# Retention and a tanh-shrink MLP on one core: the first eight steps in another hand-written order

## The chip, the core and the metric

The kernel runs on one core of a Trainium2 chip. The core has a matrix engine (TensorE, PE in the profile, with its weight loads shown as PEld), three engines for elementwise work (VectorE, DVE; ScalarE, ACT; GpSimd, POOL) and a sync engine (SP) that here only issues DMAs. Every engine works off its own instruction list in order and waits for others by semaphores. The metric is the device time of one launch in microseconds (us), smaller is better. With the kernel before, four runs had a median of 696.73 us (695.07 to 699.09).

## The reference

```python
# q, k, v: (4, 8, 768, 64); w_in: (512, 2048); w_out: (2048, 512)
def _attn_ref(q, k, v):
    B, H, S, D = q.shape
    gamma = 1.0 - 2.0 ** (-5.0 - np.arange(H, dtype=np.float32))
    scale = 1.0 / np.sqrt(D)
    state = np.zeros((B, H, D, D), dtype=np.float32)
    y = np.zeros_like(q)
    for t in range(S):
        state = gamma[None, :, None, None] * state + np.einsum('bhd,bhe->bhde', k[:, :, t], v[:, :, t])
        y[:, :, t] = scale * np.einsum('bhd,bhde->bhe', q[:, :, t], state)
    return y.astype(np.float32)

# x: attention output as (3072, 512)
def _moe_ref(x, w_in, w_out):
    h = x @ w_in
    g = h - np.tanh(h)
    return (g @ w_out).astype(np.float32)
```

All inputs and the output are float32 or wider; the weights arrive as 64-bit floats and are converted on the chip.

## The kernel before

The 3072 tokens are 24 chunks of 128 (six chunks to a batch element). Each chunk goes through the attention in chunked form: powers of gamma are multiplied into q and v, k and q are transposed, products of k with v (the state's increment) and of k with q (the scores) are formed, the scores are masked, and outputs are summed from state and scores in PSUM and copied to `xT`, the transposed input of the MLP. The MLP runs in steps: a step is a pair (n, m2), 256 tokens by 256 columns of the hidden layer. It has an up-projection (two halves of 128 hidden columns), a chain of elementwise work for h - tanh(h) (a polynomial where h is small, and a choice between the two), and a down-projection (two halves of 128 tokens). Weights come in 32 blocks, alternating four blocks of w_in and four of w_out; each is loaded as 64-bit words and turned into float32 by bit operations on VectorE, ScalarE and GpSimd.

From step 8 on a loop sets the order, and from step 32 on both projections use a form with seven products in place of eight. The first eight steps are different: with them go the attention of chunks 0 to 7, the loads of chunks 0 to 8, and the conversion of weight blocks 0 to 11. Their order is a string of 367 single operations, `order` (lines 892 to 913), that is worked off from left to right; `pieces` (line 858) says what each name calls. Since every engine keeps the order in which its instructions are written, the string fixes the order on each engine and on SP's queue. The number behind the colon is a chunk c, a weight block i or a step s, and a last letter D, P or A gives VectorE, GpSimd or ScalarE as the engine.

- SP: `Lk Lq Lv` load k, q, v of a chunk (lines 255, 260; one DMA of 256 KB); `W` loads a weight block (line 154 for w_out, one DMA of 512 KB; line 159 for w_in, three DMAs). There are two buffers for k, two for q and four for v, given out in the order of the loads, so a load can wait in the queue until the older user of its buffer is done.
- TensorE: `x` sets a number of warm-up blocks of 128 columns that the next piece writes first (line 233); `t`, `T` transpose k and q (298); `p` makes the products, the k-v half at line 343, the scores at 349; `b` makes the outputs from state and scores (398), `r` the rest of them; `u`, `v` are the two halves of an up-projection (464); `o0`, `o1` those of a down-projection (531).
- VectorE: `z`, `Z` the two halves of the state (367 to 373), `m` the mask (356), `D1` to `D4` the bit operations of a weight block (191 to 201), `f0` to `f4` the products of the shrink (844 to 854).
- ScalarE: `c`, `C` copy the transposes out (310, 307), `e` copies four single columns of the outputs to `seen` (428), which `r` then waits for, `y` copies the outputs to `xT` (444), `A`, `l` take the high and low words of a weight block (175, 183), `au` to `alarge` the functions of the shrink (836), `E` keeps a finished half of a down-projection (545).
- VectorE or GpSimd: `s`, `w` multiply the powers of gamma into q and v (282), `F`, `G` end the conversion of a weight block (208, 217). A block is converted in the order A, l, D1 to D4, F, G.

What waits for what, where it matters here: `T` needs `s`, the first half of `p` needs `w` and k, its second half `c` and `C`; `b` needs `z` and `m` of its chunk; `u` and `v` of a step need `y` of its two chunks and `G` of one block each; `o` needs `f4` and `G` of two blocks.

Of the kernel before, what the change touches and what calls it, by code (L numbers as in the profile page):

```python
# [22 lines left out]
A = 0.00694305119022808  # L23
# [8 lines left out]
def kernel(  # L32
# [857 lines left out]
    if w_out.dtype != F32:  # L890
        rooms += [xp.tile([P, 2, 2 * BANK], U32, tag="xT", name=f"raws_{i}") for i in range(3)]
    order = """
    Lk:0 Lq:0 s:0D x:9 t:0 c:0 Lv:0 x:3 T:0 C:0 Lk:1 Lq:1 w:0D p:0 W:0 Lv:1 t:1 z:0 s:1P Z:0
    m:0 x:2 b:0 Lq:2 Lv:2 Lq:3 e:0 w:1D s:2D c:1 A:0 T:1 Lk:2 C:1 r:0 x:1 p:1 D1:0 z:1 T:2 m:1
    s:3D D2:0 Z:1 y:0 b:1 t:2 W:1 Lk:3 e:1 w:2P r:1 D3:0 C:2 l:0 c:2 p:2 D4:0 F:0P G:0P Lv:3
    y:1 z:2 m:2 A:1 T:3 b:2 t:3 Z:2 D1:1 D2:1 l:1 D3:1 D4:1 u:0 W:3 Lq:4 c:3 W:2 Lk:4 e:2 C:3
    r:2 y:2 w:3P p:3 l:3 A:3 Lv:4 F:1D z:3 Lv:5 Lq:5 Lk:5 m:3 G:1P b:3 s:4P e:3 A:2 v:0 r:3
    Z:3 D1:3 D2:3 w:4P W:5 Lv:6 ath:0 y:3 au:0 T:4 t:4 c:4 C:4 aq0:0 D3:3 D1:2 aq1:0 D4:3 D2:2
    alarge:0 l:2 F:3P f0:0 D3:2 v:2 p:4 f1:0 u:2 f2:0 s:5P G:3P au:2 ath:2 Lq:6 z:4 m:4 aq0:2
    Z:4 t:5 T:5 c:5 C:5 f3:0 Lk:6 A:5 D4:2 f4:0 w:5D F:2D f0:2 f1:2 D1:5 G:2P v:1 b:4 s:6P  # L900
    aq1:2 f2:2 w:6P p:5 e:4 r:4 z:5 f3:2 m:5 D2:5 u:1 W:4 D3:5 y:4 T:6 A:4 l:5 t:6 v:3 D1:4
    D4:5 D2:4 b:5 F:5D W:6 Lq:7 c:6 C:6 ath:1 l:4 D3:4 au:1 G:5D D4:4 e:5 aq0:1 p:6 r:5
    alarge:1 aq1:1 y:5 alarge:2 A:6 Lv:7 Lk:7 F:4D W:7 W:8 u:3 G:4P W:11 W:9 W:10 o0:0 s:7P
    m:6 f0:1 z:6 Z:6 f1:1 Lq:8 au:3 f4:2 D1:6 f2:1 A:7 aq0:3 t:7 D1:7 o1:0 T:7 f3:1 v:4 u:4
    l:6 aq1:3 D2:6 b:6 C:7 c:7 D2:7 f4:1 D3:6 ath:3 f0:3 D4:6 f1:3 w:7P f2:3 f3:3 D3:7 p:7
    F:6P G:6P e:6 l:7 D4:7 F:7D r:6 au:4 u:5 A:11 ath:4 m:7 y:6 G:7P v:5 alarge:3 f4:3 z:7
    aq1:4 au:5 aq0:4 o0:1 E0:1 f0:4 f1:4 f2:4 D1:11 o1:1 b:7 o0:2 ath:5 aq0:5 alarge:5 A:10
    aq1:5 e:7 E1:1 l:11 l:10 alarge:4 r:7 y:7 o1:2 f3:4 D2:11 Z:7 D1:10 D3:11 D2:10 D4:11
    F:11D f0:5 f1:5 f2:5 G:11D D3:10 D4:10 f4:4 f3:5 o0:3 A:8 F:10P D1:8 u:6 G:10D D2:8 v:6
    A:9 D1:9 D2:9 f4:5 D3:9 D4:9 D3:8 au:6 ath:6 aq0:6 aq1:6 E0:3 f0:6 l:9 o1:3 u:7 v:7 E1:3  # L910
    f1:6 f2:6 f3:6 D4:8 au:7 aq0:7 ath:7 alarge:6 l:8 F:9P G:9P f0:7 o0:4 aq1:7 F:8P o1:4 o0:5
    o1:5 E0:5 alarge:7 Lk:8 Lv:8 W:12 f4:6 f1:7 W:13 f2:7 f3:7 G:8D f4:7 W:14 E1:5
    """
    for piece in order.split():
        kind, at_ = piece.split(":")
# [200 lines left out]
```

## Time and profile before

| what | value |
|---|---|
| median of 4 runs | 696.73 us (695.07 to 699.09) |
| the profiled execution, its own time | 695.07 us |
| its span in the profile | 693.2 us |
| instructions | 16487 |
| first matmul of step 8 | 85.47 us after the span's start |
| granted TensorE clock in every stretch of 20 us | 1.00 |
| DMA, mean over the span | 86 GB/s (59.95 MB) |

The span is what the profiler sees between the first and the last instruction; the time has some 1.9 us around it. A share of busy time is a mean over the whole span, and the first eight steps are only its first eighth: the views by window and the timeline are the ones to read here. In a line of the timeline stand start and length in us, engine, line of the kernel, operation, the tiles written and read, their shape and the number of instructions, and in brackets the idle time of the engine before it with what ended that. Matmuls overlap each other, so their cost is read from start to start.

### The profile page before, as it was taken

The numbers are of one execution on the slowest core, as the hardware profiler recorded it, in microseconds if no ns is written. First come the engines' busy times: TensorE is split into PE (matmuls) and PEld (weight loads), VectorE is DVE, ScalarE is ACT, GpSimd is POOL, SyncE is SP. The second block draws the span as 40 slices with busy tenths as digits, with TensorE's granted clock in tenths as the row PEclk, the third lists the DMA queues.
The fourth block names the chain that finished last, engine by engine and source line by source line (L and its number), as shares of the span: only waits on it lengthen the run. The fifth ranks groups of instructions, "written<-read, shape, count | busy, mean of one in ns | idle before, by whom it ended". The sixth has DMA issues, their size and how long they took to land.

```text
span 693.2 us, 16487 instructions
## 1 busy us (share of the span) xinstructions
PE 686.1 (99%) x6540; PEld 572.7 (83%) x6540; DVE 524.0 (76%) x894; ACT 432.5 (62%) x818; POOL 347.7 (50%) x517
## 2 busy tenths in 40 slices
PE   8999999999999999999999999999999999999997
PEld 6776666667666767789999999999999999999996
DVE  4899999988988965487777676677676776766775
ACT  3787677767767665555665555655556655556653
POOL 1632454455544767878753354453544543544333
PEclk9999999999999999999999999999999999999999
DMA  9991278878968566400000000000000000000001
GB/s 237 239 293 48 66 181 223 206 175 243 210 189 228 143 162 192 124 32 1 1 1 22 11 1 31 1 1 31 1 1 31 1 8 24 2 16 17 1 16 46
DMA packets 119548, 59.95 MB, mean 86 GB/s; under 512 B 101680, under 2 KB 112560, under 8 KB 119472
## 3 DMA queue, kind: packets, MB, share of 16 engines
q1 hardware_dynamic: 116880, 50.21, 28.0%
q10 hardware_dynamic: 2592, 8.69, 3.4%
q8 instruction: 51, 0.84, 0.5%
q14 instruction: 25, 0.20, 0.1%
HBM read 35.83 MB, written 14.68 MB: 73 GB/s over the span
## 4 chain that ended last, share of the span: by engine, by line
PE 95%; DVE 1%; SPq 1%; issue 1%; DMA 1%; ACT 1%; POOL 0%; POOLq 0%; DVEq 0%; ACTq 0%
PE h L778 29%; PE h L464 16%; PE o L531 16%; PE fast_t L669 10%; PE y L669 8%; PE fast_o L669 8%; PE y L398 4%; PE s L349 2%; PE s L343 2%; PE kqTp L298 1%; DMA v<-in_v_dram 1%; SPq L260 0%; SPq L255 0%; SPq L159 0%; DVE g L523 0%
## 5 line engine op out<-in xcount | busy, mean ns | idle before, releaser
L477 ACT ACTIVATE th<-h 128x512 f32<-128x512 f32 x64 | 38.2, 598 | 141.5 <-DVE h L795 141.5
L620 POOL TENSOR_TENSOR s<-g 128x128 f32<-128x128 f32 x64 | 29.3, 457 | 192.2 <-DVE g L523 186.4
L464 PE MATMUL h<-xT,w 128*128 128x256 f32 x512 | 117.7, 382 | 0.0
L531 PE MATMUL o<-w,g 128*128 128x512 f32 x256 | 116.5, 596 | 0.0
L464 PEld LDWEIGHTS h<-xT,w 128*128 128x128 f32 x512 | 95.9, 190 | 21.3 <-issue 9.1
L531 PEld LDWEIGHTS o<-w,g 128*128 128x128 f32 x256 | 47.5, 190 | 46.2 <-issue 43.0
L778 PEld LDWEIGHTS h<-xT,w 128*128 128x128 f32 x512 | 76.8, 191 | 8.4 <-ACT fast_head L783 1.0
L523 DVE COPY_PREDICATED g<-large,th 128x512 f32<-128x512 int32 x88 | 74.0, 841 | 8.9
L793 DVE TENSOR_TENSOR h<-h,fast_head 128x256 f32<-128x256 f32 x64 | 27.7, 432 | 68.1 <-PE h L778 66.9
L778 PE MATMUL h<-xT,w 128*128 128x128 f32 x512 | 78.3, 275 | 0.2 <-ACT fast_head L783 0.2
L502 DVE TENSOR_TENSOR th<-h,th 128x512 f32<-128x512 f32 x88 | 60.1, 683 | 17.5 <-ACT th L475 16.2
L515 DVE SCALAR_TENSOR_TENSOR g<-q,h 128x512 f32<-128x512 f32 x64 | 44.0, 688 | 36.3 <-ACT q L491 34.8
L778 PE MATMUL h<-x,w 128*128 128x128 f32 x448 | 68.3, 275 | 0.0
L483 ACT ACTIVATE q<-u,tab 128x512 f32<-128x512 f32 x88 | 63.8, 725 | 1.8
L491 ACT ACTIVATE q<-u,tab 128x512 f32<-128x512 f32 x88 | 63.6, 723 | 0.0
L506 DVE SCALAR_TENSOR_TENSOR h<-q,h 128x512 f32<-128x512 f32 x88 | 60.8, 691 | 2.6 <-ACT q L483 2.6
L208 POOL TENSOR_TENSOR low<-low,power 128x512 f32<-128x512 f32 x26 | 34.6, 1330 | 56.1 <-DVE power L201 48.4
L492 ACT ACTIVATE large<-u,tab 128x512 f32<-128x512 f32 x88 | 62.6, 712 | 0.0
L778 PEld LDWEIGHTS h<-x,w 128*128 128x128 f32 x448 | 59.0, 192 | 0.0
L783 ACT COPY fast_head<-h 128x512 f32<-128x512 f32 x64 | 37.5, 586 | 20.3 <-PE h L778 20.3
L522 DVE TENSOR_TENSOR g<-g,u 128x512 f32<-128x512 f32 x64 | 49.1, 768 | 0.0
L788 POOL TENSOR_TENSOR fast_head<-fast_head 128x256 f32<-128x256 f32 x64 | 46.8, 731 | 1.2 <-ACT fast_head L783 1.2
(197 smaller groups left out, 1496.6 us busy)
## 6 DMA issues: line engine op xcount, KB each, us to landing
rows<-apart ACTq DMA_DIRECT2D x16, 512.0 KB, 4.8
k<-in_k_dram SPq DMA_DIRECT2D x24, 256.0 KB, 4.2
q<-in_q_dram SPq DMA_DIRECT2D x24, 256.0 KB, 4.8
v<-in_v_dram SPq DMA_DIRECT2D x24, 256.0 KB, 5.6
raw<-in_moe_w_out_dram SPq DMA_DIRECT2D x12, 512.0 KB, 4.6
out_dram<-sum SPq DMA_DIRECT2D x22, 256.0 KB, 2.0
raw<-in_moe_w_in_dram SPq DMA_DIRECT2D x14, 256.0 KB, 4.1
raw<-in_moe_w_in_dram SPq DMA_DIRECT2D x28, 128.0 KB, 3.9
```

The costliest lines, as they stand in the source:

```text
L464: nc.tensor.matmul(hp, w1[:, c, ts(2 * m2 + i, P)], xT[n // 2][:, c, ts(n % 2, TH)], start=(begins and c == 0), stop=(c == NC - 1), skip_g ...
L483: nc.scalar.activation(q0, shrinking[n, m2][0], AF.Square, bias=bias0)
L491: nc.scalar.activation(q1, u, AF.Square, bias=bias1, scale=math.sqrt(A))
L492: nc.scalar.activation(large, u, AF.Relu, bias=bias_m)
L502: nc.vector.tensor_tensor(th, hp, th, op=ALU.subtract)
L506: nc.vector.scalar_tensor_tensor(hp, in0=shrinking[n, m2][2], scalar=C0, in1=hp, op0=ALU.add, op1=ALU.mult)
L522: nc.vector.tensor_tensor(flat, src, u, op=ALU.mult)
L523: nc.vector.copy_predicated(flat, large.bitcast(I32), th)
L531: nc.tensor.matmul(o_p[n, j], gT[n, m2][:, i, ts(j, P)], w2[:, 2 * m2 + i], start=(first and i == 0), stop=(last and i == 1))
L669: nc.tensor.matmul(accs[n][k], left[k - 1], right, start=first and k in (1, 6, 7, 4), stop=last, skip_group_check=True)
L778: nc.tensor.matmul(hps[n, m2][:, ts(PLACE[k], P)], s_of[m2][k - 1][:, c], x_of[n][k - 1][:, c], start=(k == 1 and c == 0), stop=(c == 1), ...
L788: nc.gpsimd.tensor_tensor(odd_room[1], first[:, :2], first[:, 3:1:-1], op=ALU.add)
```

## The change

The string `order` is replaced by another with the same 367 operations. Their places differ, and some go to another queue or engine: `Lk:0` from SP's queue to ScalarE's; `s:1 s:7 w:3 w:4 F:6 F:9 F:10 G:0 G:1` from GpSimd to VectorE; `w:5 F:2 F:4 F:5 F:7 G:5 G:10` from VectorE to GpSimd. Nothing else in the kernel is touched.

```diff
--- before.py
+++ after.py
@@ -890,26 +890,26 @@
     if w_out.dtype != F32:
         rooms += [xp.tile([P, 2, 2 * BANK], U32, tag="xT", name=f"raws_{i}") for i in range(3)]
     order = """
-    Lk:0 Lq:0 s:0D x:9 t:0 c:0 Lv:0 x:3 T:0 C:0 Lk:1 Lq:1 w:0D p:0 W:0 Lv:1 t:1 z:0 s:1P Z:0
-    m:0 x:2 b:0 Lq:2 Lv:2 Lq:3 e:0 w:1D s:2D c:1 A:0 T:1 Lk:2 C:1 r:0 x:1 p:1 D1:0 z:1 T:2 m:1
-    s:3D D2:0 Z:1 y:0 b:1 t:2 W:1 Lk:3 e:1 w:2P r:1 D3:0 C:2 l:0 c:2 p:2 D4:0 F:0P G:0P Lv:3
-    y:1 z:2 m:2 A:1 T:3 b:2 t:3 Z:2 D1:1 D2:1 l:1 D3:1 D4:1 u:0 W:3 Lq:4 c:3 W:2 Lk:4 e:2 C:3
-    r:2 y:2 w:3P p:3 l:3 A:3 Lv:4 F:1D z:3 Lv:5 Lq:5 Lk:5 m:3 G:1P b:3 s:4P e:3 A:2 v:0 r:3
-    Z:3 D1:3 D2:3 w:4P W:5 Lv:6 ath:0 y:3 au:0 T:4 t:4 c:4 C:4 aq0:0 D3:3 D1:2 aq1:0 D4:3 D2:2
-    alarge:0 l:2 F:3P f0:0 D3:2 v:2 p:4 f1:0 u:2 f2:0 s:5P G:3P au:2 ath:2 Lq:6 z:4 m:4 aq0:2
-    Z:4 t:5 T:5 c:5 C:5 f3:0 Lk:6 A:5 D4:2 f4:0 w:5D F:2D f0:2 f1:2 D1:5 G:2P v:1 b:4 s:6P
-    aq1:2 f2:2 w:6P p:5 e:4 r:4 z:5 f3:2 m:5 D2:5 u:1 W:4 D3:5 y:4 T:6 A:4 l:5 t:6 v:3 D1:4
-    D4:5 D2:4 b:5 F:5D W:6 Lq:7 c:6 C:6 ath:1 l:4 D3:4 au:1 G:5D D4:4 e:5 aq0:1 p:6 r:5
-    alarge:1 aq1:1 y:5 alarge:2 A:6 Lv:7 Lk:7 F:4D W:7 W:8 u:3 G:4P W:11 W:9 W:10 o0:0 s:7P
-    m:6 f0:1 z:6 Z:6 f1:1 Lq:8 au:3 f4:2 D1:6 f2:1 A:7 aq0:3 t:7 D1:7 o1:0 T:7 f3:1 v:4 u:4
-    l:6 aq1:3 D2:6 b:6 C:7 c:7 D2:7 f4:1 D3:6 ath:3 f0:3 D4:6 f1:3 w:7P f2:3 f3:3 D3:7 p:7
-    F:6P G:6P e:6 l:7 D4:7 F:7D r:6 au:4 u:5 A:11 ath:4 m:7 y:6 G:7P v:5 alarge:3 f4:3 z:7
-    aq1:4 au:5 aq0:4 o0:1 E0:1 f0:4 f1:4 f2:4 D1:11 o1:1 b:7 o0:2 ath:5 aq0:5 alarge:5 A:10
-    aq1:5 e:7 E1:1 l:11 l:10 alarge:4 r:7 y:7 o1:2 f3:4 D2:11 Z:7 D1:10 D3:11 D2:10 D4:11
-    F:11D f0:5 f1:5 f2:5 G:11D D3:10 D4:10 f4:4 f3:5 o0:3 A:8 F:10P D1:8 u:6 G:10D D2:8 v:6
-    A:9 D1:9 D2:9 f4:5 D3:9 D4:9 D3:8 au:6 ath:6 aq0:6 aq1:6 E0:3 f0:6 l:9 o1:3 u:7 v:7 E1:3
-    f1:6 f2:6 f3:6 D4:8 au:7 aq0:7 ath:7 alarge:6 l:8 F:9P G:9P f0:7 o0:4 aq1:7 F:8P o1:4 o0:5
-    o1:5 E0:5 alarge:7 Lk:8 Lv:8 W:12 f4:6 f1:7 W:13 f2:7 f3:7 G:8D f4:7 W:14 E1:5
+    Lq:0 Lk:0A x:9 t:0 Lv:0 c:0 Lv:1 Lk:1 s:0D x:3 T:0 C:0 w:0D Lq:2 p:0 Lq:1 W:0 z:0 W:1 Lv:2
+    m:0 x:2 b:0 e:0 t:1 Z:0 w:1D c:1 s:1D Lk:2 r:0 s:2D y:0 T:1 C:1 A:0 w:2P x:1 p:1 z:1 D1:0
+    Lq:3 D2:0 T:2 m:1 b:1 A:1 C:2 Lk:3 l:1 e:1 Lv:3 t:2 c:2 Z:1 D3:0 r:1 D1:1 l:0 D2:1 p:2
+    D4:0 F:0P s:3D m:2 z:2 D3:1 G:0D w:3D T:3 Z:2 D4:1 F:1D y:1 b:2 e:2 C:3 t:3 W:3 Lq:4 s:4P
+    W:2 Lk:4 c:3 G:1D u:0 A:3 D1:3 r:2 y:2 A:2 p:3 z:3 Lv:4 m:3 Z:3 v:0 D2:3 D1:2 D2:2 T:4
+    D3:3 D3:2 t:4 C:4 w:4D c:4 b:3 D4:3 e:3 D4:2 l:3 r:3 y:3 Lq:5 au:0 aq1:0 ath:0 p:4 v:2
+    Lk:5 F:3P z:4 Lv:5 W:5 s:5P W:7 Z:4 m:4 f0:0 G:3P Lk:6 w:5P alarge:0 aq0:0 t:5 A:5 T:5 c:5
+    u:2 Lv:6 Lq:6 l:2 F:2P W:4 f1:0 b:4 G:2P C:5 p:5 s:6P f2:0 D1:5 f3:0 e:4 ath:2 au:2 r:4
+    f4:0 z:5 aq1:2 aq0:2 m:5 f0:2 Lq:7 Lk:7 W:11 Lv:7 W:6 W:10 W:9 Lq:8 Lv:8 y:4 W:8 w:6P v:1
+    A:4 t:6 T:6 D2:5 f1:2 u:1 C:6 D3:5 D1:4 c:6 l:5 b:5 D4:5 D2:4 F:5P f2:2 au:1 p:6 e:5 f3:2
+    D3:4 r:5 m:6 G:5P D4:4 z:6 aq1:1 y:5 l:4 F:4P G:4P Z:6 alarge:2 alarge:1 s:7D aq0:1 ath:1
+    v:3 u:3 T:7 t:7 o1:0 f4:2 f0:1 o0:0 w:7P A:7 D1:7 D2:7 f1:1 l:7 c:7 C:7 ath:3 au:3 b:6
+    D3:7 f2:1 A:6 aq0:3 D1:6 f3:1 aq1:3 e:6 p:7 r:6 D4:7 f0:3 f1:3 u:4 z:7 f2:3 F:7P Z:7 D2:6
+    f3:3 D3:6 v:4 f4:1 l:6 au:4 u:5 y:6 m:7 alarge:3 D4:6 G:7P b:7 F:6D G:6P ath:4 A:11 v:5
+    e:7 r:7 o1:1 o0:1 D1:11 aq1:4 alarge:4 aq0:4 A:10 l:10 au:5 E1:1 f0:4 l:11 y:7 f1:4 D1:10
+    o0:2 D2:11 D2:10 D3:10 D4:10 f2:4 f3:4 f4:3 D3:11 D4:11 E0:1 o1:2 aq0:5 alarge:5 ath:5
+    aq1:5 F:11D G:11D f0:5 f1:5 f2:5 f3:5 F:10D A:9 G:10P f4:4 v:7 u:7 o1:3 D1:9 ath:7 au:7
+    A:8 f0:7 D2:9 l:8 f4:5 D3:9 D1:8 D2:8 alarge:7 o0:3 E0:3 l:9 aq0:7 v:6 E1:3 D3:8 u:6 f1:7
+    D4:9 D4:8 o1:4 aq1:7 au:6 ath:6 aq0:6 F:9D f0:6 f2:7 aq1:6 o0:4 o1:5 f1:6 Lk:8 W:12 W:13
+    F:8P o0:5 E1:5 G:8D alarge:6 W:14 f3:7 f2:6 f3:6 f4:7 f4:6 G:9P E0:5
     """
     for piece in order.split():
         kind, at_ = piece.split(":")
```

Taken apart, the beginnings of four of the lists (old, then new):

```
SP      Lk0 Lq0 Lv0 Lk1 Lq1 W0 Lv1 Lq2 Lv2 Lq3 Lk2 W1 Lk3 Lv3 W3 Lq4 W2 Lk4 Lv4 Lv5 Lq5 Lk5 W5 Lv6 Lq6 Lk6 W4
        Lq0 Lv0 Lv1 Lk1 Lq2 Lq1 W0 W1 Lv2 Lk2 Lq3 Lk3 Lv3 W3 Lq4 W2 Lk4 Lv4 Lq5 Lk5 Lv5 W5 W7 Lk6 Lv6 Lq6 W4
TensorE x9 t0 x3 T0 p0 t1 x2 b0 T1 r0 x1 p1 T2 b1 t2 r1 p2 T3 b2 t3 u0 r2 p3 b3 v0 r3 T4 t4 v2 p4 u2 t5 T5 v1 b4 p5 r4 u1 T6 t6
        x9 t0 x3 T0 p0 x2 b0 t1 r0 T1 x1 p1 T2 b1 t2 r1 p2 T3 b2 t3 u0 r2 p3 v0 T4 t4 b3 r3 p4 v2 t5 T5 u2 b4 p5 r4 v1 t6 T6 u1
ScalarE c0 C0 e0 c1 A0 C1 y0 e1 C2 l0 c2 y1 A1 l1 c3 e2 C3 y2
        c0 C0 e0 c1 y0 C1 A0 A1 C2 l1 e1 c2 l0 y1 e2 C3 c3 A3 y2
VectorE s0 w0 z0 Z0 m0 w1 s2 D1:0 z1 m1 s3 D2:0 Z1 D3:0 D4:0 z2 m2 Z2 D1:1
        s0 w0 z0 m0 Z0 w1 s1 s2 z1 D1:0 D2:0 m1 Z1 D3:0 D1:1 D2:1 D4:0 s3 m2 z2 D3:1 G0 w3 Z2
```

## The prediction

> **What bounds the kernel now.** I read the engines' busy shares first, then the shares of the chain that ended last.
>
> ```profile
> PE 686.1 (99%) x6540; PEld 572.7 (83%) x6540; DVE 524.0 (76%) x894; ACT 432.5 (62%) x818; POOL 347.7 (50%) x517
> ...
> PE 95%; DVE 1%; SPq 1%; issue 1%; DMA 1%; ACT 1%; POOL 0%; POOLq 0%; DVEq 0%; ACTq 0%
> ```
>
> TensorE is the bound, so an order can only take away or add time in which TensorE waits. The windows show where such time can be (stretch, its length, then busy us and instructions of PE, PEld, DVE, ACT, POOL, then granted clock, DMA share, GB/s):
>
> ```profile
> 0.00:20.00 20.00, 17.50 (x393) 12.48 (x393) 9.83 (x20) 8.93 (x23) 4.81 (x8) 1.00 0.90 233
> 20.00:40.00 20.00, 19.60 (x409) 16.26 (x406) 18.49 (x34) 15.30 (x40) 11.99 (x11) 1.00 0.97 271
> 40.00:60.00 20.00, 20.00 (x314) 16.00 (x314) 19.15 (x34) 15.89 (x37) 7.11 (x6) 1.00 0.68 181
> 60.00:80.00 20.00, 20.00 (x124) 12.08 (x123) 18.46 (x35) 14.11 (x29) 3.85 (x3) 1.00 0.21 70
> ```
>
> For 40 us the DMA engines are full: the load order is a queue for one resource. From 20 us on VectorE is nearly full too. TensorE's waits:
>
> ```profile
> PE kqTp L233 <- DVE w L116: 1.4, 1, 1.4
> PE s L349 <- ACT kqT L310: 0.7, 1, 0.7
> PE y L398 <- DVE state L369: 0.3, 1, 0.3
> PE y L398 <- DVE a L356: 0.2, 1, 0.2
> ```
>
> From the timeline, the issue of W:1, the copy c:2, the second half of p:2 that waits for it, the outputs b:3, and w:4 on GpSimd:
>
> ```profile
> 11.54 2.77 SPq L159 DMA_DIRECT2D raw<-in_moe_w_in_dram  x3
> ...
> 17.11 0.57 ACT L310 COPY kqT<-kqTp 128x512 f32<-128x512 f32 x1
> ...
> 17.73 0.69 PE L349 MATMUL s<-kqT 64*64 64x64 f32 x32 [0.69 <-ACT kqT L310]
> ...
> 24.23 0.46 PE L398 MATMUL y<-kqT,state 64*64 64x64 f32 x16 [0.26 <-DVE state L369]
> ...
> 28.59 1.04 POOL L282 TENSOR_TENSOR v<-v,tab 128x512 f32<-128x512 f32 x1 [2.73 <-DMA v<-in_v_dram]
> ```
>
> **How much there is to win.** Step 8's first matmul starts at 85.47 us. I add up the TensorE work before it at its pace when nothing is waited for (start to start): 64 transposes of 0.109, 128 up matmuls of 0.216, 48 down matmuls of 0.430, 32 small ones in 0.46, 15 warm-up blocks of 0.107. With the warm-up counted twice, as each of its blocks is two instructions, that is 72.75 us. TensorE started at 1.45, so 11.3 us are over: 2.5 by 6.9 us (the cold start: a 512-column matmul took 853 ns there, half as much later), 4.8 from there to u:0 at 20.46, 2.8 to 46.53, 1.1 after that. Most of it is the 0.15 to 0.2 us of each change between small and large matmuls, which every order pays. Two pieces stand out, 0.91 over at p:2 and 0.86 over at b:3. More than about 2.5 us cannot be had.
>
> **The change, step by step.** The operations are the same 367; queues and engines differ. Landing times of before come from the trace's landing records: k:0 4.59, v:0 6.33, k:1 7.26, q:1 8.02, W:0 10.62, v:1 11.67, v:2 13.86, q:3 14.51, k:2 15.35, W:1 18.48, k:3 19.02, q:4 23.17, W:2 25.42. So a k or v costs the stream about 1.1 us, a q 0.85, a weight block 1.7 or more. Durations start to start: VectorE 0.60 for a product of two tiles, 0.35 for a bit operation or half a state; ScalarE 0.5 to 0.6 a copy; GpSimd 1.04 a scale, 1.27 an F or G.
>
> *Start, to 8.8 us: 0.* k:0 goes to ScalarE's queue behind the table (issue 0.43 us), q:0 is first on SP. TensorE's warm-up ends at 5.45 either way, and k:0 needs to land by then; alone on its queue, issued at 1.2 with before's 3.85 us, it lands at 5.0. ScalarE has nothing before c:0 at 6.45. If it lands 0.5 late, 0.5 is lost.
> The Trainium skill, "DMA: Bandwidth & Descriptors", section "Queues, rings and completion order", says the rows of the queues are served in turn by the same 16 engines, so a second queue adds no bandwidth; by that rule k:0 would share with v:0 and land some 0.5 us later than on a queue of its own, where the trace of before has only the table on that queue.
>
> *q:2 before q:1.* There are two q buffers; q:1 now waits in SP's queue for s:0 (over at 6.2), with W:0, W:1 and all later loads behind it. q:2's issue ahead fills SP until about 5.4, so this costs under 0.8, and nothing while the stream has a backlog.
>
> *p:1: -0.3.* v:1 lands at 7.3 in place of 11.67; q:1 at about 10.4. w:1, s:1 on VectorE end at 11.7, T:1 at 12.2, C:1 12.9, p:1's second half starts at 12.9 against 13.15.
>
> *b:1 to p:2: +0.5.* z:1, D1:0, D2:0, m:1 stand in a row on VectorE: 13.6+0.35+0.35+0.35+0.68 = 15.35, so b:1 ends at 15.7 (before 15.45). W:1's three DMAs now stand before v:2, k:2 and q:3 on SP: those land at 15.1, 16.2, 17.1 at the costs above, 17 for k:2 by the pace after 15 us. t:2 ran at 15.48, now 16.3. On ScalarE A:1 stands before C:2, l:1, e:1, c:2; with W:1 at 15.2 they end at 17.9, p:2 at 18.5 against 18.36.
>
> *u:0 and p:3: +0.45 in all.* m:2 now precedes z:2, so b:2 waits until 19.6; t:3 ends at 20.6. G:0 on VectorE (0.60 instead of 1.27) follows s:3, m:2, z:2, D3:1 and ends at 20.8: u:0 at 20.9 against 20.46, p:3 at 23.0 against 22.56.
>
> *b:3: -0.86, then +0.4 and up to 0.8.* v:0, T:4 and t:4 now lie between p:3 and b:3, so the wait for state and mask is covered. But r:3 now follows b:3 with nothing between, and must wait for the four copies e:3 (0.45). Behind it p:4 waits for w:4, now on VectorE, with D4:3, D4:2, z:4 queued behind it: v:4 landed at 28.5 before and should at 27 to 28.5. At the end of v:2 (p:4 included on both sides) I get 31.1 to 31.9 against 31.4.
>
> *T:6: 0 to +1.* q:6 lands at 36 to 38 (34.9 before), as W:7 and two others now precede it; s:6 takes 1.04 on GpSimd, while TensorE arrives at 38.0. u:1 ends at 40.4 to 41.5 against 40.86.
>
> *The rest: 0 to +0.5.* Nine products move to VectorE and seven off it: +2 x 0.60, at 0.60 and 1.27 each; VectorE has 1 to 2 us in 20 to spare. o:0 needs G:4 at about 46 to 47.6 with TensorE there at 46.4 to 48; o:1 needs G:6 at 58.6 with TensorE there at 59.8. At the end f:4 of step 6 is last on VectorE, at about 85; it is needed one up-projection after step 8 begins, at 88. Were that cover gone, step 8's down-projection would wait by the difference.
>
> **Sum:** -0.3 +0.5 +0.25 -0.86 +0.8 (middle of 0.4 to 1.2) lands at +0.4; T:6 and the rest could add, hidden covers could take: I use +0.3. The profiled span 693.2 becomes 693.5, its run 695.07 becomes 695.4. That run was the fastest of four; on the median 696.73 this is 697.0.
>
> **Rivals.**
> *Late W:1, slower.* In the trace W:1 landed at 18.48 although it was issued from 11.54. If splitting and back pressure hold it there, A:1 starts at 18.5, C:2, l:1, e:1 and c:2 end at 21.2, and p:2's second half starts at 21.25 in place of 17.73; k:2 behind W:1 would land at 20.5 and gives the same. That is +3.5 to +4: 700.2 to 700.7. It decides from a landing after 15.2 on, us for us. Against it: the 512 KB stands two loads earlier in a full stream. Chance 0.15.
> *The waits go away, faster.* p:2 and b:3 lose their 0.9 each, later loads run 1 us ahead and r:3 is hidden: -1.7, 695.0. For it: the loads behind W:1 keep their order and start issue about 1 us earlier. Chance 0.2; still within 0.5%.
> *The clock falls.* TensorE idles more between 14 and 17 us. No row of before shows the clock falling once granted (1.00 in every stretch). The cold start cost 2.4 us in 4.7; as much again gives 699.4. Chance 0.05.
> The Trainium skill, "TensorE: Matmul & The Clock Gate", section "Part 1: The HAM clock gate (the "warmup" mystery)", has the clock halve after an idle window of some 3.4 us; no gap I find is half that, so by the rule the clock stays.
> *Order does nothing:* loads are hidden anyway. It is part of the forecast.
>
> **Numbers.** My forecast (-1 to +2) has 0.55, the rivals 0.15, 0.2, 0.05, and 0.05 is for a lost cover that I did not find, some +4. About 0.5% (3.5 us) is what a measurement of this kernel can tell from no change. Slower by that: the late half of W:1's rival, the unfound one and a part of the forecast's upper tail: 0.16. Faster by that exceeds what there is to win: 0.03. Range: below by 2.2 (the possible win), above by 4 (late W:1): 694.5 to 700.7.
>
> **What would show it.** Step 8's first matmul between 84.5 and 87.5; TensorE's wait at p:2 or t:2 kept or grown, none at b:3, a new one at r:3 on the copies to seen, one for w:4 or s:6 on landings. A first TensorE matmul of step 8 after 89, a wait of over 2 us, or TensorE gaps beyond step 8 would make me wrong.

## The result, and the profile after

The changed kernel takes 698.78 us (median of 42 runs, 696.62 to 703.60) where the kernel before takes 696.33 us (67 runs, 694.36 to 699.31). The ratio is 1.0034 with an interval of 1.0027 to 1.0041: 2.4 us slower. (The 67 runs include the four from which the 696.73 us ahead of the prediction came.) The profiled execution took 698.03 us, its span is 696.2 us.

The page's busy shares, for the whole span:

```profile
PE 686.3 (99%) x6540; PEld 572.8 (82%) x6540; DVE 528.3 (76%) x896; ACT 433.2 (62%) x818; POOL 347.9 (50%) x515
PE 90%; DVE 5%; ACT 2%; DMA 2%; issue 1%; POOL 0%; POOLq 0%; DVEq 0%; ACTq 0%
```

TensorE did the same work (686.3 against 686.1 us). In the chain that ended last VectorE's share went from 1% to 5%. The windows say where (columns as before: stretch, length, busy us of PE, PEld, DVE, ACT, POOL, clock, DMA share, GB/s):

```profile
0.00:20.00 20.00, 16.67 (x359) 11.89 (x360) 11.23 (x22) 8.91 (x23) 3.10 (x6) 1.00 0.90 226
20.00:40.00 20.00, 18.71 (x447) 15.75 (x440) 17.67 (x32) 14.31 (x38) 9.85 (x10) 1.00 0.93 265
40.00:60.00 20.00, 19.36 (x310) 14.99 (x308) 19.90 (x34) 14.81 (x36) 10.66 (x8) 1.00 0.72 194
60.00:80.00 20.00, 20.00 (x127) 12.61 (x126) 18.80 (x31) 15.46 (x32) 2.94 (x2) 1.00 0.16 53
```

TensorE lost 0.83, 0.89 and 0.64 us of busy time in the first three windows and none in the fourth; the clock stayed at 1.00. From the timeline, the pieces that waited (start, length, the operation, and in brackets the wait ahead of it and what ended it):

```profile
15.60 0.46 PE L398 MATMUL y<-a,v 64*64 64x64 f32 x16 [0.43 <-DVE a L356]
16.72 0.63 PE L298 MATMUL kqTp<-tab,k 128*128 128x128 f32 x4 [0.66 <-DMA k<-in_k_dram]
...
19.20 0.63 PE L298 MATMUL kqTp<-tab,wide 128*128 128x128 f32 x4 [0.48 <-DVE wide L282]
...
29.34 0.46 PE L398 MATMUL y<-a,v 64*64 64x64 f32 x16 [0.70 <-ACT seen L428]
30.26 0.69 PE L343 MATMUL s<-v,k 64*64 64x64 f32 x32 [0.46 <-DVE v L282]
...
48.81 0.63 PE L298 MATMUL kqTp<-tab,wide 128*128 128x128 f32 x4 [0.64 <-DVE wide L282]
```

In order: b:1 waits for its mask, t:2 for k:2's landing, T:3 for s:3, r:3 for the copies e:3, p:4 for w:4, T:7 for s:7. The lateness against the kernel before, read at the starts of the same pieces (or, where their order differs, where the same set is done), grows in three places:

| up to | before | after | late by |
|---|---|---|---|
| p:1 done | 13.78 | 13.59 | -0.19 |
| t:2 | 15.48 | 16.72 | 1.24 |
| p:2's second half | 17.73 | 18.04 | 0.31 |
| u:0 | 20.46 | 21.40 | 0.94 |
| p:3 | 22.56 | 23.61 | 1.05 |
| v:2, p:4 and all ahead of them done | 31.46 | 33.18 | 1.72 |
| u:1, v:1, t:6, T:6 done | 40.86 | 42.43 | 1.57 |
| o0:0, o1:0, T:7, t:7 and all ahead of them done | 50.84 | 53.49 | 2.65 |
| step 8 | 85.47 | 88.08 | 2.61 |

So some 0.9 us went before u:0 (0.3 up to p:2, as most of t:2's lateness replaces the wait that the kernel before has at p:2), 0.8 between there and v:2, 1.1 at T:7 and the down-projection behind it; from there to step 8 nothing. These are one execution of each kernel. After step 8 the profiles differ by one wait of 0.4 us for a transposed load at 121 us.

One more view separates the two. Between 35 and 50 us, before and then after:

```profile
35.00:50.00 15.00, 15.00 (x306) 11.66 (x305) 14.78 (x29) 13.29 (x33) 6.76 (x6) 1.00 1.01 299
```

```profile
35.00:50.00 15.00, 14.36 (x310) 12.15 (x309) 14.90 (x22) 13.40 (x33) 10.93 (x10) 1.00 1.04 289
```

VectorE is full in both, but 22 of its operations run in these 15 us in place of 29. Some are simply longer. The first two lines here are VectorE's, the other two GpSimd's, all of after:

```profile
36.08 1.80 DVE L854 COPY_PREDICATED g<-large,th 128x512 f32<-128x512 int32 x1
43.97 1.80 DVE L197 SCALAR_TENSOR_TENSOR head<-raws,head 128x512 uint32<-128x512 uint32 x1
```

```profile
36.00 1.27 POOL L208 TENSOR_TENSOR low<-low,power 128x512 f32<-128x512 f32 x1 [0.84 <-ACT low L183]
43.95 1.27 POOL L217 TENSOR_TENSOR w<-low,head 128x512 f32<-128x512 f32 x1
```

The two operations take 0.74 and 0.69 us where nothing runs beside them. Started just behind a product on GpSimd, each lasted until that product was over and some 0.6 us more. Added up, operations beyond their undisturbed length by over 0.1 us, VectorE was held up for 4.6 us between 35 and 50 us (0.7 before), and for 8.6 us in the first 88 us (4.1 before). The Trainium skill ("SBUF — State Buffer", section "SBUF: two separate sides") calls this an exclusive lock on a port pair that the two engines share, held for the whole instruction; it has it for VectorE operations in a 2-port mode or with two inputs in SBUF. These lines agree, and so does what was not held up. In the first 88 us of the fourteen profiles of this document, 193 VectorE operations that have all their operands in SBUF (the bit operations, f4, the products) began beside a GpSimd product: 171 of them took over 0.1 us more than alone, and the other 22 began in its last 0.25 us. Of 356 that read PSUM (z, Z, m, f0 to f3) none took over 0.04 us more.

### The profile page after: what moved, and what is told of

Same layout as the page of the kernel before. It is cut to its first block, busy times and chain, and to the rows that moved or that the text cites. A ratio compares the mean times of both kernels' runs of the same rounds, so it can differ in the third digit from the quotient of the medians.

```text
span 696.2 us, 16486 instructions
## 1 busy us (share of the span) xinstructions
PE 686.3 (99%) x6540; PEld 572.8 (82%) x6540; DVE 528.3 (76%) x896; ACT 433.2 (62%) x818; POOL 347.9 (50%) x515
## 4 chain that ended last, share of the span: by engine, by line
PE 90%; DVE 5%; ACT 2%; DMA 2%; issue 1%; POOL 0%; POOLq 0%; DVEq 0%; ACTq 0%
PE h L778 28%; PE o L531 15%; PE h L464 14%; PE fast_t L669 10%; PE y L669 8%; PE fast_o L669 8%; PE y L398 3%; PE s L349 1%; PE s L343 1%; DMA rows<-apart 1%; PE kqTp L233 1%; PE kqTp L298 1%; DMA kqT<-rows 1%; DVE head L197 1%; DVE a L356 1%
## 5 line engine op out<-in xcount | busy, mean ns | idle before, releaser
L523 DVE COPY_PREDICATED g<-large,th 128x512 f32<-128x512 int32 x88 | 76.1, 865 | 10.0 <-DVE g L522 0.9
```

The source lines that it names most:

```text
L523: nc.vector.copy_predicated(flat, large.bitcast(I32), th)
```

## The experiments

Each kernel was measured in 4 to 12 executions, with the kernel before on the same chip beside it (medians 696.10, 696.46 and 696.35 us in the three sets); the ratios are to these. The start of T:0 tells how a profile's own beginning fell: the clock rose to full at 4.5 to 7.7 us from the span's start, another value in each execution. Compare step 8's start with that in mind.

| kernel | median us | ratio to before, interval | T:0 | step 8 |
|---|---|---|---|---|
| before | 696.33 | 1 | 6.89 | 85.47 |
| after | 698.78 | 1.0034 [1.0027, 1.0041] | 6.93 | 88.08 |
| e1_engines_back | 702.51 | 1.0091 [1.0073, 1.0109] | 6.87 | 94.17 |
| e2_loads_back | 703.15 | 1.0100 [1.0087, 1.0113] | 6.68 | 92.70 |
| e3_mask_first | 700.39 | 1.0052 [1.0037, 1.0068] | 7.04 | 90.42 |
| e4_k2_first | 698.47 | 1.0036 [1.0024, 1.0049] | 7.66 | 88.57 |
| f1_early_fixed | 699.00 | 1.0034 [1.0020, 1.0048] | 7.53 | 88.55 |
| f2_r3_filled | 698.93 | 1.0031 [1.0021, 1.0041] | 7.43 | 87.99 |
| f3_o_fixed | 698.36 | 1.0033 [1.0018, 1.0048] | 6.54 | 87.72 |
| f4_all_fixed | 699.43 | 1.0040 [1.0026, 1.0053] | 6.74 | 89.79 |
| g1_seven_back | 700.99 | 1.0072 [1.0058, 1.0086] | 6.73 | 91.33 |
| g2_before_seven | 699.75 | 1.0048 [1.0037, 1.0060] | 6.05 | 90.19 |
| g3_before_loads | 699.19 | 1.0046 [1.0028, 1.0063] | 7.41 | 87.98 |
| g4_before_both | 700.33 | 1.0054 [1.0040, 1.0067] | 6.57 | 89.94 |

**First set: one part undone.** The new order with all sixteen moved products back on their old engines:

```diff
- s:1D s:7D w:3D w:4D F:6D F:9D F:10D G:0D G:1D   w:5P F:2P F:4P F:5P F:7P G:5P G:10P
+ s:1P s:7P w:3P w:4P F:6P F:9P F:10P G:0P G:1P   w:5D F:2D F:4D F:5D F:7D G:5D G:10D
```

> The new order with all 16 products back on the engines that they had before (nine to GpSimd, seven to VectorE). Theory (four local waits of TensorE: b:1 and t:2 on m:1 and k:2, 1.4 us; r:3 and p:4, 0.7 us; T:7 and o:1 on s:7 and G:4, 1.1 us; less 0.2 at p:1): only the last of these is touched for the better, and u:0 and p:3 get later as G:0 and w:3 take 1.27 and 1.04 us on GpSimd. 698 to 700 us, step 8 at 87.5 to 89.5 us. Rival 1 (VectorE has too much, by the nine products and by waiting behind GpSimd): back to 696.3 us, step 8 at 85.5.

It became 3.7 us slower than the changed kernel, above both expectations. Two lines of TensorE's waits (us in total, times, longest):

```profile
PE kqTp L298 <- POOL wide L282: 2.2, 1, 2.2
PE h L464 <- POOL w L217: 1.9, 2, 1.4
```

T:7 now waits for s:7 on GpSimd, up-projections for G:0 and G:1 there. All three are among the nine products that the change had moved to VectorE. So the sixteen moves together are not the loss: without them the new order is slower still.

The new order with the old sequence of loads (only k:0 stays on ScalarE's queue):

```diff
- Lq:0 Lk:0A Lv:0 Lv:1 Lk:1 Lq:2 Lq:1 W:0 W:1 Lv:2 Lk:2 Lq:3 ...
+ Lq:0 Lk:0A Lv:0 Lk:1 Lq:1 W:0 Lv:1 Lq:2 Lv:2 Lq:3 Lk:2 W:1 ...
```

> The new order with the loads in the sequence of before on SP's queue (only k:0 stays on ScalarE's). Theory: k:2 lands at 15.4 and t:2 no longer waits, but W:1 lands at about 18.5 while A:1 still stands ahead of C:2, e:1 and c:2 on ScalarE, so p:2's second half starts at about 21 in place of 18.04: 700 to 702 us, step 8 at 90 to 91. Rival 2 (the loads' order is the whole loss): 696.3 us, step 8 at 85.5.

It lost 7.0 us against before, above the 700 to 702 us expected. From the timeline, ScalarE's A:1, TensorE's r:1, and below them three windows, cut where the clock stepped:

```profile
19.60 0.66 ACT L175 ACTIVATE head<-raw 128x512 f32<-128x512 f32 x1 [5.23 <-DMA raw<-in_moe_w_in_dram]
```

```profile
21.68 0.70 PE L398 MATMUL y<-a,v 64*64 64x64 f32 x16 [4.15 <-ACT seen L428]
```

```profile
15.71:19.12 3.41, 1.09 (x24) 0.74 (x20) 1.65 (x4) 0.00 (x0) 0.00 (x0) 1.00 1.02 271
19.12:22.54 3.42, 0.85 (x32) 0.86 (x36) 1.79 (x4) 2.89 (x9) 0.00 (x0) 0.50 0.81 221
22.54:25.95 3.41, 3.41 (x96) 2.96 (x92) 1.77 (x3) 0.81 (x3) 2.32 (x2) 0.50 0.86 248
```

A:1 stands early in ScalarE's list. With W:1 late it holds the engine for 5.23 us, e:1 and c:2 behind it, TensorE waits 4.15 us, and then runs 6.8 us at half clock. This is the mechanism of the rival *Late W:1*, with a price above the one I gave it, in a kernel that really has W:1 late. In the changed kernel W:1 landed at 15.05, and it did not occur; A:1 starts 4.5 us earlier there:

```profile
15.15 0.67 ACT L175 ACTIVATE head<-raw 128x512 f32<-128x512 f32 x1 [1.66 <-DMA raw<-in_moe_w_in_dram]
```

The mask ahead of the bit operations (`D1:0 D2:0` from before `m:1` to behind `Z:1`), and k:2 ahead of W:1:

```diff
- z:1 D1:0 Lq:3 D2:0 T:2 m:1 b:1 ... t:2 c:2 Z:1 D3:0
+ z:1 Lq:3 T:2 m:1 b:1 ... t:2 c:2 Z:1 D1:0 D2:0 D3:0
```

> D1:0 and D2:0 behind m:1 and Z:1 on VectorE, nothing else. Theory: b:1 ends 0.8 us earlier, but t:2 waits for k:2's landing at 16.6 all the same: no change, 698.8 us within 0.4, step 8 at 87.7 to 88.3; t:2 waits 1.3 us in place of 0.7. Rival 3 (each wait counts by itself): -0.8 us, 698.0, step 8 at 87.3.

```diff
- W:0 z:0 W:1 Lv:2 m:0 ... s:1D Lk:2 r:0
+ W:0 z:0 Lk:2 W:1 Lv:2 m:0 ... s:1D r:0
```

> k:2's load ahead of W:1 and v:2 on SP's queue, nothing else. Theory: t:2's wait of 0.7 us goes, but W:1 and v:2 land 1.1 us later, and so do A:1, D1:1, s:3 and w:2, which T:3 and p:2 wait for: -0.3 to +0.5 us, 698.5 to 699.3. Rival 3: -0.7 us, 698.1, step 8 at 87.4.

With the mask first t:2 started at 16.48 instead of 16.72, and then waited for k:2, as that was the later of the two. T:3, which waits for s:3, came no earlier (19.32; 19.20 in the changed kernel). The time was expected to stay at 698.8 us; it is 700.39 us, and in the profile p:5 lost 2 us. ScalarE's and TensorE's lines there:

```profile
36.36 0.67 ACT L175 ACTIVATE head<-raws 128x512 f32<-128x512 f32 x1 [2.55 <-DMA raws<-in_moe_w_out_dram]
```

```profile
38.64 0.69 PE L343 MATMUL s<-v,k 64*64 64x64 f32 x32 [1.97 <-issue]
```

W:5 landed at 35.93 (33.41 in the changed kernel), and A:5 stands ahead of both copies of chunk 5; "issue" only says that the wait is not resolved in the trace. The list ahead of the prediction has only w and k for this half of p, but p:5 starts 0.1 us after C:5, the second copy, ended at 38.54. Why W:5 came late, and whether it did so in the other executions, is not known. With k:2 first the time did not change (698.47 us), as expected. k:2 landed at 13.54, and t:2 no longer waited for it; T:3 waited 0.55 for s:3 instead. Counted from T:0, t:2 started 0.7 us earlier than in the changed kernel, T:3 only 0.3.

**Second set: three repairs.** f1 takes both of these edits, puts A:1 and l:1 behind c:2 and s:3 before D1:1; f2 fills the gap ahead of r:3 and takes w:4 forward; f3 takes the last products ahead of o0:0 and o1:0 off GpSimd and puts o1:0 ahead of T:7 and t:7; f4 is all three.

```diff
f1
- Lk:2 (behind s:1D)  D1:0 D2:0 (before m:1)  A:1 (before C:2)  s:3D (behind F:0P)
+ Lk:2 (before W:1)   D1:0 D2:0 (behind Z:1)  A:1 (behind c:2)  s:3D (before D1:1)
f2
- v:0 D2:3 D1:2 D2:2 T:4 D3:3 D3:2 t:4 C:4 w:4D c:4 b:3 D4:3 e:3
+ v:0 D2:3 D1:2 b:3 e:3 T:4 t:4 ... w:4D (before D3:2)
f3
- D4:4 ... l:4 F:4P G:4P ... T:7 t:7 o1:0
+ l:4 D4:4 F:4D G:4D ... o1:0 T:7 t:7
```

> All that holds chunks 1 to 3 back at once: k:2's load ahead of W:1, m:1 ahead of D1:0 and D2:0, s:3 ahead of D1:1 on VectorE, A:1 and l:1 behind c:2 on ScalarE. Theory (the waits mask each other; only together do they give): u:0 at 20.2 to 20.6 in place of 21.4, step 8 at 86.9 to 87.3, 697.5 to 698.0 us. Rival (the landings after 17 us set the pace whatever the order): u:0 at 21.2 to 21.6, 698.8 us.

> b:3 and e:3 ahead of T:4 and t:4, so that these lie between b:3 and r:3, and w:4 ahead of D3:2 on VectorE; nothing else. Theory: r:3 no longer waits for the copies, p:4 starts at 29.3 to 29.7 in place of 30.26, step 8 at 87.2 to 87.5, 698.0 us. Rival (p:4 waits for v:4's landing, r:3's wait is hidden under it): p:4 at 30.0 to 30.3, no change, 698.8.

> F:4 and G:4 on VectorE right behind D4:4, and o1:0 ahead of T:7 on TensorE; nothing else. Theory: o1:0 starts right behind u:3 at 47.9 in place of 49.86, T:7 and t:7 at 49.6, step 8 at 87.0 to 87.4, 697.7 us. Rival (VectorE is the bound there, two more products on it cost as much as GpSimd's chain did): step 8 at 88, 698.8 or above.

> The three edits before together. Theory (the three stretches count separately): step 8 at 85.3 to 86.0, 696.0 to 696.7 us, as the kernel before. Rival (what is won early is waited for later, as the loads set T:6 and o:1): step 8 at 86.5 to 87.3, 697.5 us or above.

Each moved the piece it aimed at, and none moved the time by more than its uncertainty, where 0.8 to 2.8 us less than the changed kernel were expected. In f1 t:2 starts at 15.80, then p:2 waits for w:2, which waits for the later v:2:

```profile
18.16 0.69 PE L343 MATMUL s<-v,k 64*64 64x64 f32 x32 [1.21 <-POOL v L282]
```

In f2 r:3 no longer waits, and p:4 starts 0.5 us earlier, with 0.77 us of wait for the copy c:4 left in front of it. In f3 o1:0 starts at 47.49 (49.86 in the changed kernel, whose T:0 was 0.4 later), VectorE's hold-up between 35 and 50 us falls from 4.6 to 2.7 us, and then r:6 pays:

```profile
47.49 1.98 PE L531 MATMUL o<-w,g 128*128 128x512 f32 x4 [0.41 <-DVE w L217]
...
54.60 0.46 PE L398 MATMUL y<-a,v 64*64 64x64 f32 x16 [0.98 <-ACT seen L428]
```

f4 has a wait of 1.9 us at p:2 and then 3.4 us at half clock.

**Third set: the parts exchanged.** After two theories had fallen, one was left that named GpSimd: the seven products moved there hold VectorE up, and the early loads do the rest. It is tested from both sides.

```diff
g1, in the changed order
- w:5P F:2P F:4P F:5P F:7P G:5P G:10P
+ w:5D F:2D F:4D F:5D F:7D G:5D G:10D
g2, in the order before
- w:5D F:2D F:4D F:5D F:7D G:5D G:10D
+ w:5P F:2P F:4P F:5P F:7P G:5P G:10P
g3, in the order before (g4: g2 and g3 together)
- Lk:0 Lq:0 Lv:0 Lk:1 Lq:1 W:0 Lv:1 Lq:2 Lv:2 Lq:3 Lk:2 W:1
+ Lq:0 Lk:0A Lv:0 Lv:1 Lk:1 Lq:2 Lq:1 W:0 W:1 Lv:2 Lk:2 Lq:3
```

> The changed order as it is, with the seven products w:5, F:2, F:4, F:5, F:7, G:5 and G:10, which the change moved to GpSimd, back on VectorE. Theory (GpSimd's products hold VectorE's operations up between 35 and 50 us): in the trace of the changed kernel VectorE's operations there take 4.6 us more than alone (0.7 in the kernel before); with the seven back this falls below 1.5 us, o:1 starts 1 us or more before 49.86, step 8's first matmul is at 86.5 to 87.5 instead of 88.1, and the time is 697.3 to 698.3 where the changed kernel has 698.8. Rival (VectorE's own count of operations is the bound there): seven operations of 0.60 more on VectorE, step 8 at 88 to 90, 698.8 to 701.

The theory fell, the rival held: 700.99 us. The hold-up did go, from 4.6 to 1.6 us, but VectorE has seven more operations in its list, and waits of its own in them. VectorE, then TensorE:

```profile
35.83 0.69 DVE L208 TENSOR_TENSOR low<-low,power 128x512 f32<-128x512 f32 x1 [1.24 <-ACT low L183]
```

```profile
38.93 1.97 PE L464 MATMUL h<-xT,w 128*128 128x256 f32 x8 [1.08 <-DVE g L851]
...
51.26 0.63 PE L298 MATMUL kqTp<-tab,wide 128*128 128x128 f32 x4 [1.34 <-DVE wide L282]
```

F:2 waits 1.24 us for l:2, and all of VectorE's list behind it. On GpSimd, in the changed kernel, the same product waited 0.84 us and VectorE's list went on; there it costs by stretching f4, as the lines of 36.00 and 36.08 above show.

> The kernel before, with the same seven products moved from VectorE to GpSimd and nothing else. Theory: VectorE is held up by 2 us or more between 35 and 50 us, step 8's first matmul is at 86.5 to 88 (85.5 in the kernel before), time +1 to +2.5, 697.5 to 699. Rival (they are hidden in any order): step 8 within 0.5 us of 85.5 and a ratio of 0.999 to 1.001.

> The kernel before, with its first twelve loads alone in the changed sequence (k:0 on ScalarE's queue, v:1 early, q:2 ahead of q:1, W:0 and W:1 ahead of v:2, k:2, q:3). Theory (the early load order is the other part of the loss): k:2 lands at 16.3 to 16.9 instead of 15.4, t:2 waits for it some 0.5 to 1 us, step 8's first matmul at 86 to 87, 696.8 to 698. Rival (loads are hidden): step 8 within 0.3 us of 85.5, the time unchanged. In a third case W:1 holds q:3 or k:3 up and the loss is over 2 us.

> The kernel before with both: the seven products on GpSimd and the first twelve loads in the changed sequence. Theory (these two make the whole loss): about the sum of the two, step 8 at 87.5 to 89, 698 to 699.5. Rival (the order of TensorE's and ScalarE's operations is what costs): under half of the changed kernel's loss, below 697.6.

The seven alone cost the old order 3.4 us, more than the 1 to 2.5 expected, and not where expected. In the profile VectorE is held up for 2.4 us between 35 and 50 us, but TensorE's only new wait after 20 us is one for G:4, last in a row of products on GpSimd:

```profile
51.16 1.98 PE L531 MATMUL o<-w,g 128*128 128x512 f32 x4 [1.08 <-POOL w L217]
```

Another 3.4 us of that profile came from 13.7 us on, before any of the seven: q:2 landed at 15.02, T:2 waited 2.2 us for it, and the clock was half for 6.8 us. The five other executions show a mean clock of 0.999 or 1.000 and still took 698.97 to 700.10 us; where they lost it no profile shows.

The loads alone cost 2.8 us, the third case of the expectation, by q:3. VectorE's line, and TensorE's p:2:

```profile
17.47 0.69 DVE L282 TENSOR_TENSOR wide<-q,tab 128x512 f32<-128x512 f32 x1 [2.02 <-DMA q<-in_q_dram]
18.08 0.42 DVE L194 TENSOR_SCALAR head<-head 128x512 uint32<-128x512 uint32 x1
18.42 0.42 DVE L373 TENSOR_TENSOR state<-s,state 128x256 f32<-128x256 f32 x1
```

```profile
16.74 0.63 PE L298 MATMUL kqTp<-tab,k 128*128 128x128 f32 x4 [0.78 <-DMA k<-in_k_dram]
...
18.98 0.69 PE L343 MATMUL s<-v,k 64*64 64x64 f32 x32 [1.22 <-DVE state L373]
```

q:3 lands at 17.38 (14.51 before). s:3 waits for it, D2:0 and the state Z:1 stand behind s:3, and p:2 waits for Z:1, which reads the scores (line 373). The changed order has s:3 behind Z:1 on VectorE. So it is made for its loads, as the old order is for its own: e2 is the same misfit the other way round, at A:1.

Both together were expected to give the sum and came out above both expectations, yet are not the sum (6.2 us) but 4.0, and not the loss of the changed kernel (2.4) either. Every mixture of the two orders that was run (e1, e2, g1 to g4) has a median above both of theirs, though the intervals of g2, g3 and g4 reach that of the change. No kernel here beats the one before. The order of the pieces alone, with both the old engines and the old loads, was not run.

## Why the prediction came out as it did

The sign was right, the sum too small: 697.0 was predicted, +0.3 us of change, and 698.78 came, +2.4. That is inside the range, but above the forecast of -1 to +2. The range reached further for the sake of the late W:1, which did not occur, so it is in part luck that the time fell inside it. In the profile the sum's own measure, step 8's first matmul, is +2.61, at 88.08 instead of between 84.5 and 87.5. Taken by what each stretch added to the lateness, three terms of the sum were too small, by 0.5, 0.7 and 1.1 us, and the others were right:

- *Start: 0.* k:0 landed at 5.14 (5.0 was worked out), T:0 started at 6.93 against 6.89. Right.
- *p:1: -0.3.* p:1 ended 0.19 earlier. Right.
- *b:1 to p:2: +0.5.* The three causes were there: b:1 waited for its mask until 15.60 (15.35 was worked out), k:2 landed at 16.59 (16.2 to 17), W:1 at 15.05 (15.2). t:2 came 1.24 late against 0.8 worked out, but p:2's second half, which waited 0.69 in the kernel before, now did not wait: from 0.19 early to 0.31 late is +0.50. Right.
- *u:0 and p:3: +0.25 in the sum (+0.45 with what came before).* Mis-sized: 0.94 and 1.05 late, which is 0.6 to 0.7 more than at p:2. VectorE's bit operation D1:1 took 1.27 us (from 16.40) instead of 0.42, beside w:2 on GpSimd. Behind it in VectorE's list stand s:3, for which T:3 waited 0.48, and G:0, which ended at 21.35 where 20.8 was worked out; u:0 started at 21.40.
- *b:3: -0.86, then +0.4 to +1.2.* b:3's wait went, and the two waits named in its place came: r:3 for the copies (0.70, not 0.45) and p:4 for w:4 (0.46, behind bit operations on VectorE: v:4 had landed at 28.69, w:4 started at 29.43). Mis-sized: the sum took 0.8 for the two, which makes -0.06 for the stretch; they waited 1.16, and from p:3 to the end of v:2 the lateness grew by 0.67.
- *T:6: 0 to +1.* Nothing was lost between v:2 and T:6 (1.72 late, then 1.57). Right, at the low end.
- *The rest: 0 to +0.5, none of it in the sum.* Mis-sized: measured +1.1, at T:7 and o1:0. The working priced a product at 0.60 us on VectorE and 1.27 on GpSimd and summed VectorE's load from these; it put at nothing that the two stretch each other, by which VectorE lost 8.6 us of the first 88 in place of 4.1. T:7 waited 0.64 for s:7, which took 0.6 us more than alone beside F:4 on GpSimd (the line below), and o1:0 began at 49.86, just after G:4 had ended on GpSimd at 49.81.

```profile
47.41 1.25 DVE L282 TENSOR_TENSOR wide<-q,tab 128x512 f32<-128x512 f32 x1
```

In f3, with F:4 and G:4 on VectorE, o1:0 starts 2 us earlier; but f3 also puts it ahead of T:7 and t:7, and what each of the two edits gave is not separated. That the total follows from this place is not shown: in f3 the time did not.

Of the rivals, *late W:1* did not occur, as W:1 landed at 15.05; e2 shows that its mechanism is real. *The waits go away* was half right: those at p:2 and b:3 went, others came. *The clock falls* did not occur in the profiled run of the change, but did in the profiles of five of the twelve experiments, at waits of 1.9 to 4.2 us. It seems to come in some executions of the changed kernel too: its two slowest, 703.60 and 701.38 us, have a mean clock of 0.995 and 0.996, where the others have 0.998 to 1.000 and e2, with 6.8 us at half clock, has 0.995. An execution of the kernel before, beside the third set, has 699.76 us and 0.995. The reason given against this rival fits the profiled run, whose longest wait behind the start is 0.70 us; but a whole idle window is not needed, as waits of 1.9 to 2.2 us were enough in e1, f4, g2 and g4. Of the signs named in advance, the wait at t:2 and the new ones at r:3 and p:4 came; a gap of TensorE beyond step 8, which was to count against the prediction, came as well, but is only the 0.4 us at 121 us.

The places of the loss are shown; one cause behind the 2.4 us is not. Each repair uncovered another wait: that VectorE, ScalarE and the loads are all due at nearly the same time is how I read it, which no run shows, and which of them is the last was not found. Also, why the seven products cost the old order as much as they do in the executions with a full clock stays open.

## What to carry to other kernels

In an order written for engines that work in sequence, find for each instruction that waits for a landing what stands behind it on its engine, and price that: s:3 and A:1 each had TensorE wait 1 to 4 us in an order made for other loads; in their own, no wait of TensorE goes back to those landings. Do not judge half of such a change by the whole, or improve it wait by wait when several engines are full at once; undo and redo parts from both sides, since a mixture can be worse than either. When VectorE is full, price a product that is moved to GpSimd by what it adds to the VectorE operations it overlaps (here those with all operands in SBUF), not by its own length.

## What the runs showed of the hardware

*The clock falls after a window that is about half idle.* It stepped only at multiples of 3.41 us from its own first rise. In those windows at full clock in the first 88 us in which TensorE was busy for 1.09 (e2), 1.25 (e1), 1.46 (g4), 1.52 (f4) and 1.81 us (g2), the next window ran at 0.5; after 1.89 (e3), 1.95 (e4), 1.97 (g1) and more it stayed at 1.0. Two pairs, g2 and e3:

```profile
11.28:14.70 3.42, 1.81 (x82) 1.42 (x74) 0.69 (x1) 1.91 (x5) 0.00 (x0) 1.00 1.01 252
14.70:18.11 3.41, 2.22 (x48) 1.92 (x52) 3.06 (x7) 0.00 (x0) 1.11 (x1) 0.50 0.58 165
```

```profile
37.12:40.53 3.41, 1.89 (x83) 1.80 (x84) 2.36 (x5) 3.34 (x10) 2.31 (x2) 1.00 0.73 239
40.53:43.95 3.42, 3.42 (x21) 2.87 (x20) 3.42 (x5) 2.80 (x7) 2.97 (x3) 1.00 1.03 303
```

So a wait of 2 us can cost a half-speed window or nothing, by where it falls. The bound between 1.81 and 1.89 us rests on one window on each side, in one program, and on busy time whose ends of matmuls are modelled. The Trainium skill ("TensorE: Matmul & The Clock Gate", section "Part 1: The HAM clock gate (the "warmup" mystery)") names an idle window of some 3.4 us as the condition. The length of the window agrees. If the window is to be idle throughout, that does not: in these runs one with 1.81 us of work in it was enough.
